# Transposing only the filled partitions: a recurrent attention block with a sparse feed-forward block on one core

## The chip, the cores and the metric

The kernel runs on one core of a Trainium2 chip. The metric is the device time of one execution in microseconds (us), the median of several; lower is better. The profile below is one profiled execution of the same kernel. Its span, from the first to the last instruction, is a little shorter than the device time. Engines are named as the profile names them: PE is TensorE, PEld its weight loads, DVE is VectorE, ACT is ScalarE, POOL is GpSimd, and SPq and ACTq are queues that issue transfers.

## What is computed

The reference runs a decayed outer-product recurrence over 768 steps for 4 batches of 8 heads with head width 48, lays the heads side by side as 384 channels, and passes 128 of each batch's 768 tokens through a two-layer block of hidden width 1024. Cut to what matters:

```python
def _attn_ref(r, k, v, w, u):                      # r, k, v, w: (4, 8, 768, 48)
    for t in range(S):
        cur = np.einsum('bhd,bhe->bhde', u[None] * kt, vt)
        y[:, :, t] = np.einsum('bhd,bhde->bhe', rt, state + cur)
        state = wt[:, :, :, None] * state + np.einsum('bhd,bhe->bhde', kt, vt)

def _moe_ref(x, w_gate, w1, w2, capacity):         # x: (4, 768, 384), w1: (384, 1024), capacity 128
    scores = np.einsum('bsd,d->bs', x, w_gate)
    for b in range(B):
        top_idx = np.argpartition(-scores[b], capacity)[:capacity]
        xe = x[b, top_idx]
        ye = np.maximum(xe @ w1, 0.0) @ w2
        g = 1.0 / (1.0 + np.exp(-scores[b, top_idx]))
        out[b, top_idx] = x[b, top_idx] + g[:, None] * ye
```

All inputs and the output are 4-byte floats.

## The kernel before

The sequence is cut into 24 chunks of 128 tokens, six per batch. A chunk's heads are handled in four pairs (`HP = 4`). Each head takes 64 places (`DP = 64`), of which 48 (`D = 48`) hold data, so that a pair fills 128 partitions: 0 to 47 are the first head, 64 to 111 the second, and 48 to 63 and 112 to 127 are padding. The program is one list of turns; in turn `i` the engines work on chunks `i-2` to `i+2` at different stages. The order of the instructions on each engine is the order of the text.

A transpose is a product on TensorE with the data as the stationary operand and an identity matrix as the moving one. The same helper serves the way in (tokens to channels: `ps_w` for w, `ps_t` for k and r) and the way back (channels to tokens: `ps_t` of `K`, and `ps_y` of `yt`):

```python
    def transposed(pool, tag, src):
        ps = pool.tile([L, HP, L], FP32, tag=tag, name=f"ps_{tag}")
        for j in range(HP - 1, -1, -1):
            nc.tensor.transpose(ps[:, j, :], src(j), ident)       # 128 moving columns
        return ps
```

The way back for the scaled keys gives `kt`, the stationary operand of the products that carry the state:

```python
    def back(t):
        if chunks[t["n"]][1] == NCH - 1:        # a batch's last chunk carries nothing
            return
        ps = transposed(psT, "t", lambda j: t["K"][:, j, :])
        t["kt"] = lev.tile([L, HP, 2, DP], FP32, tag="kt", name="kt")
        nc.scalar.copy(out=t["kt"].rearrange("p j q d -> p j (q d)"), in_=ps)
```

The way back for the results leaves the heads of every second pair in crossed order, so that two instructions take them out:

```python
    def rows_out(t, soon=False):
        b, ci = chunks[t["n"]]
        ps = transposed(psY, "y", lambda j: t["yt"][:, j % 2, j // 2, :])
        y = ps.rearrange("p (a o) (c d) -> p o a c d", o=2, d=DP)
        ...
        for o in (0, 1):
            to = xh[:, o, :, ::-1, :] if o else xh[:, o]
            if soon:                                              # the last two chunks
                ...
                nc.vector.tensor_add(to, y[:, o, :, :, 0:D], ...)
            else:
                nc.scalar.copy(out=to, in_=y[:, o, :, :, 0:D])
        if not soon:
            nc.gpsimd.tensor_add(x, x, vo.rearrange("p h d -> p (h d)"))
        nc.sync.dma_start(out=views[b][b, ci * L:(ci + 1) * L, :], in_=x)
```

Two further helpers use TensorE at the start. `warm` multiplies zeros, and `spread` copies one row into all partitions:

```python
    def warm(n):
        ps = psM.tile([L, 512], FP32, tag="m", name="ps_n")
        for _ in range(n):
            nc.tensor.matmul(ps, nothing[:, 0:L], nothing, start=True, stop=True)

    def spread(to, row):
        ps = psM.tile([L, C], FP32, tag="m", name="ps_b")
        nc.tensor.matmul(ps, one_row, row, start=True, stop=True)
        nc.scalar.copy(out=to, in_=ps)
```

The turn, cut to the calls that the change and the prediction speak of:

```python
    def turn(i):
        soon = i >= N - 1
        ...
        step(scores, i)                    # PE: ps_s
        step(own_values, i)                # ACT: eight sums over rk
        ...
        step(masked, i)                    # DVE: sc
        step(back, i)                      # PE: ps_t <- K; ACT: kt
        if i == 0:
            warm(2)
            spread(wg_bc, wg_row)          # PE: ps_b; ACT: wg_bc
        mix(place="half")
        step(rows_out, i - 1, soon)        # PE: ps_y; ACT or DVE: x; POOL: x
        ...
        fed_in_turn(...)                   # PE: the feed-forward block of an earlier batch
        step(inputs_t, i + 1, "R", r_bufs) # PE: ps_t <- r
        step(scaled, i + 1, "R", "left")   # DVE: R
        step(decays_t, i + 2)              # PE: ps_w <- w
        mix(place="mid")
        if i == -2:
            warm(1)
        ...
        step(outputs_t, i)                 # PE: ps_yt; ACT: yt
        step(carry_products, i)            # PE: ps_kv
        fed_in_turn(...)
        step(inputs_t, i + 2, "K", k_bufs) # PE: ps_t <- k
        if not soon:
            step(row_sums, i - 1)
        step(scans, i + 2)                 # DVE: right_buf, alls, from_left, left
        ...

    warm(6)
    for i in range(-2, N + 1):
        turn(i)
    # then the selection and the feed-forward block of the last batch
```

Of the kernel before, what the change touches and what calls it, by code (L numbers as in the profile page):

```python
# [10 lines left out]
FP32 = mybir.dt.float32  # L11
# [7 lines left out]
L = 128  # L19
DP = 64  # L20
# [18 lines left out]
def kernel(  # L39
# [40 lines left out]
    nc = tc.nc  # L80
    PSUM = bass.MemoryType.PSUM

    B, H, S, D = r.shape
# [4 lines left out]
    HP = H // 2  # L88
    NDC = C // L
    NFC = F // L  # L90
    NHF = NCH // 2
    W = HP * L
    assert S % (2 * L) == 0 and C % L == 0 and F % (4 * L) == 0 and H % 2 == 0
    assert HP % 2 == 0 and D <= DP and W <= 512 and C <= 512 and 0 < CAP < S and CAP % L != 1
    assert B * NCH < 256

    consts = ctx.enter_context(tc.tile_pool(name="consts", bufs=1))
    setup = ctx.enter_context(tc.tile_pool(name="setup", bufs=1))
    lev = ctx.enter_context(tc.tile_pool(name="lev", bufs=2))
    mod = ctx.enter_context(tc.tile_pool(name="mod", bufs=1))  # L100
    psW = ctx.enter_context(tc.tile_pool(name="psW", bufs=1, space=PSUM))
    psT = ctx.enter_context(tc.tile_pool(name="psT", bufs=2, space=PSUM))
    psS = ctx.enter_context(tc.tile_pool(name="psS", bufs=1, space=PSUM))
    psY = ctx.enter_context(tc.tile_pool(name="psY", bufs=1, space=PSUM))
# [9 lines left out]
    def crossed(j, q):  # L114
        return q ^ (j & 1)
# [10 lines left out]
    for queue, hs in ((nc.sync, slice(H // 2, H)), (nc.scalar, slice(0, H // 2))):  # L126
        queue.dma_start(
            out=w_bufs[0][:, hs, 0:D], in_=w[0, hs, 0:L, :].rearrange("h t d -> t h d")
# [23 lines left out]
    def loads(n):  # L152
        load(v_bufs, v, n - 2)
        load(k_bufs, k, n - 1)
        load(r_bufs, r, n - 1)
        load(w_bufs, w, n)
# [19 lines left out]
    def load_weights(n):  # L176
        while n > 0 and weights:
            to, src = weights.pop(0)
            nc.sync.dma_start(out=to, in_=src)
            n -= 1  # L180


    ident = consts.tile([L, L], FP32)
# [7 lines left out]
    high = consts.tile([L, 1], FP32)  # L191
    nc.vector.memset(high, -HIGH)

    row = setup.tile([L, L], INT32)
    nc.gpsimd.iota(row, pattern=[[1, L]], base=0, channel_multiplier=0)
    slots = consts.tile([L, L], BF16)
# [4 lines left out]
    for t, sign in ((before_f, 1), (after_f, -1)):  # L201
        nc.gpsimd.memset(t, 1.0)
        nc.gpsimd.affine_select(
            out=t, in_=t, pattern=[[sign, L]], base=-1, channel_multiplier=-sign,
# [32 lines left out]
# [15 lines that stand above are left out]
        for j in range(HP - 1, -1, -1):  # L252
            nc.tensor.transpose(ps[:, j, :], src(j), ident)  # L253
        return ps

    def decays_t(t):
        wb = w_bufs[t["n"] % NBUF]
        t["wt"] = transposed(psW, "w", lambda j: wb[:, 2 * j:2 * j + 2, :])

    def scans(t):  # L260
# [5 lines left out]
        nc.vector.tensor_tensor_scan(  # L266
            out=flat[:, W - 2::-1], data0=wt[:, W - 1:0:-1],
            data1=from_right.rearrange("p j t -> p (j t)")[:, W - 2::-1], initial=1.0,
            op0=ALU.mult, op1=ALU.max,
# [7 lines left out]
        nc.vector.tensor_tensor_scan(  # L277
            out=left.rearrange("p j t -> p (j t)")[:, 1:W], data0=wt[:, 0:W - 1],
            data1=start.rearrange("p j t -> p (j t)")[:, 1:W], initial=start[:, 0, 0:1],
            op0=ALU.mult, op1=ALU.max,  # L280
# [6 lines left out]
    def check_sums():  # L287

        above = setup.tile([L, 1], FP32)
        nc.vector.tensor_reduce(out=above, in_=guard, axis=AX.X, op=ALU.add)  # L290
        below = setup.tile([L, 1], FP32)
        junk = setup.tile([L, N * HP], FP32)
        nc.vector.tensor_scalar(
            out=junk, in0=alls.rearrange("p n j -> p (n j)"), scalar1=float(LOW ** L),
            scalar2=None, op0=ALU.is_lt, op1=ALU.add, accum_out=below,
        )
        return above, below
# [75 lines left out]
    def back(t):  # L373
        if chunks[t["n"]][1] == NCH - 1:
            return
        ps = transposed(psT, "t", lambda j: t["K"][:, j, :])
        t["kt"] = lev.tile([L, HP, 2, DP], FP32, tag="kt", name="kt")
        nc.scalar.copy(out=t["kt"].rearrange("p j q d -> p j (q d)"), in_=ps)

    state = {}  # L380

# [25 lines left out]

    def rows_out(t, soon=False):
        b, ci = chunks[t["n"]]
        ps = transposed(psY, "y", lambda j: t["yt"][:, j % 2, j // 2, :])  # L410
        y = ps.rearrange("p (a o) (c d) -> p o a c d", o=2, d=DP)
        x = t["x"] = lev.tile([L, C], FP32, tag="x", name="x", bufs=3)
        xh = x.rearrange("p (a o q d) -> p o a q d", o=2, q=2, d=D)
        vo = t.pop("vo")
        for o in (0, 1):
            to = xh[:, o, :, ::-1, :] if o else xh[:, o]
            if soon:
                vh = vo.rearrange("p (a o q) d -> p o a q d", o=2, q=2)
                nc.vector.tensor_add(
                    to, y[:, o, :, :, 0:D], vh[:, o, :, ::-1, :] if o else vh[:, o]  # L420
                )
            else:
                nc.scalar.copy(out=to, in_=y[:, o, :, :, 0:D])  # L423
        if not soon:
            nc.gpsimd.tensor_add(x, x, vo.rearrange("p h d -> p (h d)"))  # L425
        nc.sync.dma_start(out=views[b][b, ci * L:(ci + 1) * L, :], in_=x)

    def row_products(t):
# [211 lines left out]
    def step(f, n, *more):  # L640
        if 0 <= n < N:
            f(work.setdefault(n, dict(n=n)), *more)

    def mix(n=1, place=None):


        while n > 0 and mixing:
            if place is not None and mixing[0][1] not in (None, place):
                return
            try:  # L650
                mixing[0][1] = next(mixing[0][0])
                n -= 1
            except StopIteration:
                mixing.pop(0)
# [16 lines left out]
    def fed_in_turn(n, few):  # L671

        kept = (feed or picked) and (feed or picked)[0][0] == B - 2
        fed(few if kept else n, on=False)
# [6 lines left out]
    def turn(i):  # L681
        soon = i >= N - 1
        step(first_left, i + 1)
        if i < 1:
            step(scaled_aside, i + 1, "K", "right")
        step(own_products, i + 1)
        step(scores, i)
        step(own_values, i)
        step(carry, i - 1, work.get(i))
        if i > 0:  # L690
            step(scaled, i + 1, "K", "right")
        if i >= 0:
            step(own_weights, i + 1)
        if soon:
            step(masked, i)
        if i == N - 1:
            sums.extend(check_sums())
        if i < N:
            step(compared, i - 2)
        if not soon:  # L700
            step(masked, i)
        step(back, i)
        if i == 0:
            warm(2)
            spread(wg_bc, wg_row)
        mix(place="half")
        step(rows_out, i - 1, soon)
        step(row_scores_soon if soon else row_products, i - 1)
        step(own_results, i)
        fed_in_turn(PIECES // 2, 2 if i >= N - 1 else 1)  # L710
        step(inputs_t, i + 1, "R", r_bufs)
        step(scaled, i + 1, "R", "left")
        step(decays_t, i + 2)
        mix(place="mid")
        if i == -2:
            warm(1)
        step(range_check, i + 2)
        if i == -1:
            spread(u_bc.rearrange("p h d -> p (h d)"), u_row)
            step(own_weights, i + 1)  # L720
        step(outputs_t, i)
        step(carry_products, i)
        fed_in_turn(PIECES - PIECES // 2, 1 if i == N - 1 else 0)
        if i == N - 1:
            step(compared, i - 1)
        step(inputs_t, i + 2, "K", k_bufs)
        if not soon:
            step(row_sums, i - 1)
        step(scans, i + 2)
        if 0 <= i - 2 < N - 1 and chunks[i - 2][1] == NCH - 1:  # L730
            mixing.append([mixture(chunks[i - 2][0]), "end"])
        mix(place="end")
        if i > -2:
            loads(i + 5)
        if i in WEIGHT_TURNS:
            load_weights(1)

    with tc.manual_schedule():
# [4 lines that stand above are left out]
        ended.append(True)  # L743
        mix(1000)
        mixing.append([mixture(B - 1), "half"])
        step(compared, N - 1)
        fed(1)
        mix()
        wide = checked(sums)
        fed(1)  # L750
        mix()
        fed(NFC - 2)
        mix(2)
        fed(2)
        mix(1000)
        fed(1000)
        outside = nc.values_load(wide, min_val=0, max_val=1)
# [72 lines left out]
```

## Time and profile before

| what | value |
|---|---|
| device time, three runs | 205.02, 205.38 and 209.82 us; median 205.38 us |
| span of the profiled execution | 203.5 us |
| PE busy | 190.5 us (94%) |
| DVE busy | 161.4 us (79%) |
| POOL busy | 135.5 us (67%) |
| ACT busy | 124.2 us (61%) |
| bytes moved | 28.81 MB, mean 142 GB/s |
| mean granted TensorE clock | 0.996 |

Busy time is the union of an engine's instructions. [...]PE's busy time says how seldom PE had nothing under way, and not what a product costs. That is read from how closely the starts follow each other, or from a piece of the chain of waits. The chain follows the work that ended last back to what released it, step by step; each of its pieces is named by start, duration and instruction. The windows give each engine's busy time in a chosen stretch. Shapes are written partitions x elements.

### The profile page before, as it was taken

Reading aid. Unit: us, or ns where it says so; the run is one execution under the profiler, and the core shown is the slowest. Engines: PE = TensorE matmul, PEld = TensorE weight load, DVE = VectorE, ACT = ScalarE, POOL = GpSimd, SP = SyncE. Lnnn points to the kernel's source line nnn. Section 1 sums busy time; section 2 is a strip of 40 time slices with the busy share of each in tenths; the row PEclk is TensorE's granted clock in tenths of the full one; section 3 lists DMA queues with packets and bytes.
Section 4 is the critical chain, followed back from the end, with each engine's and each line's share of the span. In section 5 each row is a group of like instructions: output and inputs, shape, how many; then the busy total and the mean of one; then the engine's idle time right before and its main releaser. Section 6 shows DMA issues by size and latency. Waiting matters only on the chain.

```text
span 203.5 us, 6413 instructions
## 1 busy us (share of the span) xinstructions
PE 190.5 (94%) x2288; PEld 154.9 (76%) x2289; DVE 161.4 (79%) x357; ACT 124.2 (61%) x642; POOL 135.5 (67%) x167
## 2 busy tenths in 40 slices
PE   6799999989899899999999999999999999999980
PEld 2478888868687788898887888898887888876940
DVE  7979999999999968988879788988879884961010
ACT  4487877768854866878354866878355866510300
POOL 6496898886857996678538898669538898111201
PEclk9999999999999999999999999999999999999998
DMA  7999999999999999798792994998872221111101
GB/s 115 163 163 150 178 192 198 243 210 213 205 216 212 259 230 208 142 244 152 137 158 68 169 183 101 151 162 150 122 116 75 46 79 39 41 42 42 39 8 43
DMA packets 105387, 28.81 MB, mean 142 GB/s; under 512 B 100482, under 2 KB 104580, under 8 KB 105348
## 3 DMA queue, kind: packets, MB, share of 16 engines
q1 hardware_dynamic: 104304, 26.65, 75.1%
q0 software_dynamic: 512, 1.57, 2.5%
q8 instruction: 20, 0.33, 0.8%
q14 instruction: 19, 0.16, 0.3%
q10 hardware_dynamic: 532, 0.10, 0.2%
HBM read 22.81 MB, written 5.51 MB: 139 GB/s over the span
## 4 chain that ended last, share of the span: by engine, by line
PE 85%; DVE 4%; DMA 3%; ACT 2%; POOL 2%; issue 2%; SPq 1%; POOLq 0%; DVEq 0%; ACTq 0%
PE ps_t L253 14%; PE ps_s L360 12%; PE ps_h L606 11%; PE ps_f L618 11%; PE ps_yt L393 11%; PE ps_w L253 5%; PE ps_yt L401 5%; PE ps_y L253 5%; PE ps_kv L455 5%; PE ps_e L496 3%; DMA w_buf<-in_w_dram 3%; PE ps_r L522 1%; PE ps_b L246 1%; ACT rk L345 1%; PE ps_x L570 1%
## 5 line engine op out<-in xcount | busy, mean ns | idle before, releaser
L345 ACT ACTIVATE rk<-rk 128x48 f32<-128x48 f32 x192 | 43.6, 230 | 0.1
L425 POOL TENSOR_TENSOR x<-x,vo 128x384 f32<-128x384 f32 x22 | 22.1, 1004 | 22.5 <-ACT x L423 22.4
L345 ACT ACTIVATION_READ_ACCUMULATOR rk<-rk 128x1 f32 x192 | 36.1, 188 | 0.0
L277 DVE TENSOR_TENSOR_SCAN left<-ps_w,from_left 128x511 f32<-128x511 f32 x24 | 30.7, 1281 | 0.9
L406 ACT COPY yt<-ps_yt 128x512 f32<-128x512 f32 x24 | 14.0, 585 | 28.0 <-PE ps_yt L401 25.2
L368 DVE TENSOR_TENSOR sc<-ps_s,before_f 128x1024 f32<-128x1024 f32 x24 | 29.3, 1219 | 0.8 <-PE ps_s L360 0.8
L266 DVE TENSOR_TENSOR_SCAN right_buf<-ps_w,from_right 128x511 f32<-128x511 f32 x24 | 29.1, 1212 | 0.8 <-PE ps_w L253 0.8
L360 PE MATMUL ps_s<-R,K 48*128 48x128 f32 x384 | 27.9, 285 | 0.3 <-ACT yt L406 0.2
L393 PE MATMUL ps_yt<-sc,v_buf 128*64 128x128 f32 x384 | 26.3, 278 | 1.4 <-PE ps_w L253 1.2
L360 PEld LDWEIGHTS ps_s<-R,K 48*128 48x128 f32 x384 | 23.3, 187 | 3.9 <-issue 2.9
L606 PE MATMUL ps_h<-xeT,w 128*128 128x128 f32 x192 | 25.5, 280 | 0.2 <-ACT hid L611 0.2
L336 POOL TENSOR_TENSOR rk<-r_buf,k_buf 128x384 f32<-128x384 f32 x24 | 24.1, 1006 | 1.3 <-DMA r_buf<-in_r_dram 1.2
L393 PEld LDWEIGHTS ps_yt<-sc,v_buf 128*64 128x64 f32 x384 | 20.6, 136 | 5.7 <-issue 2.9
L339 POOL TENSOR_TENSOR rk<-rk,u_bc 128x384 f32<-128x384 f32 x24 | 24.1, 1003 | 1.3 <-DVE alls L272 0.6
L606 PEld LDWEIGHTS ps_h<-xeT,w 128*128 128x128 f32 x192 | 22.9, 192 | 1.6 <-ACT xeT L572 0.5
L618 PE MATMUL ps_f<-w,hid 128*128 128x384 f32 x64 | 23.8, 499 | 0.0
L430 POOL TENSOR_TENSOR scr<-x,wg_bc 128x384 f32<-128x384 f32 x22 | 22.0, 1001 | 1.7
L351 POOL TENSOR_TENSOR vo<-v_buf,own 128x384 f32<-128x384 f32 x24 | 19.9, 830 | 1.3 <-ACT rk L345 1.3
L324 DVE TENSOR_TENSOR R<-ps_t,left 128x512 f32<-128x512 f32 x24 | 16.5, 687 | 5.0 <-ACT own L584 1.6
L324 DVE TENSOR_TENSOR K<-ps_t,right_buf 128x512 f32<-128x512 f32 x22 | 15.1, 685 | 4.9 <-PE ps_t L253 4.9
L253 PE MATMUL ps_w<-ident,w_buf 128*128 128x128 f32 x96 | 15.0, 278 | 1.5 <-ACT every L507 0.7
L313 ACT ACTIVATE junk<-w_buf,high 128x384 f32<-128x384 f32 x24 | 15.1, 630 | 1.0 <-DMA w_buf<-in_w_dram 0.7
(110 smaller groups left out, 348.1 us busy)
## 6 DMA issues: line engine op xcount, KB each, us to landing
k_buf<-in_k_dram SPq DMA_DIRECT2D x24, 192.0 KB, 4.2
r_buf<-in_r_dram SPq DMA_DIRECT2D x24, 192.0 KB, 4.7
v_buf<-in_v_dram SPq DMA_DIRECT2D x24, 192.0 KB, 4.9
out_dram<-x SPq DMA_DIRECT2D x24, 192.0 KB, 3.5
w_buf<-in_w_dram SPq DMA_DIRECT2D x23, 192.0 KB, 5.0
w<-in_moe_w_dram SPq DMA_DIRECT2D x3, 512.0 KB, 6.0
w<-in_moe_w_dram SPq DMA_DIRECT2D x4, 384.0 KB, 4.8
w_buf<-in_w_dram ACTq DMA_DIRECT2D x1, 96.0 KB
```

The lines of the kernel that those rows point to most:

```text
L253: nc.tensor.transpose(ps[:, j, :], src(j), ident)
L266: nc.vector.tensor_tensor_scan(out=flat[:, W - 2::-1], data0=wt[:, W - 1:0:-1], data1=from_right.rearrange("p j t -> p (j t)")[:, W - 2::- ...
L277: nc.vector.tensor_tensor_scan(out=left.rearrange("p j t -> p (j t)")[:, 1:W], data0=wt[:, 0:W - 1], data1=start.rearrange("p j t -> p (j ...
L324: nc.vector.tensor_mul(out, t.pop(name + "t"), t.pop(by))
L336: nc.gpsimd.tensor_mul(rk, r_bufs[n % NBUF][:, :, 0:D], k_bufs[n % NBUF][:, :, 0:D])
L339: nc.gpsimd.tensor_mul(t["rk"], t["rk"], u_bc)
L345: nc.scalar.activation(out=rk[:, h, :], in_=rk[:, h, :], func=AF.Copy, accum_out=o[:, h:h + 1])
L360: nc.tensor.matmul(ps[:, q, j, :], t["K"][rows, j, :], t["R"][rows, j, :], start=True, stop=True,)
L368: nc.vector.tensor_mul(t["sc"].rearrange("p q j t -> p (q j) t"), ps.rearrange("p q j t -> p (q j) t"), _heads(before_f, 2 * HP),)
L393: nc.tensor.matmul(ps[half(c), j % 2, j // 2, :], vt[:, 2 * j + q, :], t["sc"][:, q, j, :], start=(j < 2), stop=(old is None), skip_group_ ...
L606: nc.tensor.matmul(ps[:, q, :], w1[:, dc, (f0 + q) * L:(f0 + q + 1) * L], xeT[:, dc, :], start=(dc == 0), stop=(dc == NDC - 1),)
L618: nc.tensor.matmul(ps, hid[:, fc, :], w2[:, fc, :], start=(fc == 0), stop=(fc == NFC - 1))
```

## The change

Of the 128 partitions on the way back only 96 hold data, and the last data partition is 111. The change transposes partitions 0 to 111 alone (`DE = DP + D = 112`), with an identity of 112 x 112 whose columns stand in another order: the 48 columns of one head, the 48 of the other, and then the padding between. The result is 112 columns wide, and its first 96 are a pair of heads side by side. A second copy of this matrix has the two heads exchanged, for the crossed pairs. So `x` is taken out by one instruction and not by two, and `kt` by one that copies 384 elements per partition and not 512. As the padding of `kt` is no longer written, `kt` gets two fixed buffers whose padding is set to zero once.

Besides, the products of zeros are placed differently. There are none any more in turn 0 between the transposes of `K` and the row of the gate; at the start, two follow the first transposes of w and one each the first transposes of k and of r.

```diff
+    turned = consts.tile([DE, 2, DE], FP32)
+    for x in (0, 1):
+        for to, src in ((0, DP * x), (D, DP * (1 - x)), (2 * D, D)):
+            n = min(D, DE - to)
+            nc.gpsimd.tensor_copy(out=turned[:, x, to:to + n], in_=ident[0:DE, src:src + n])
+    kt_bufs = [consts.tile([L, HP, 2, DP], FP32, name=f"kt{i}") for i in range(2)]
+    for t in kt_bufs:
+        nc.gpsimd.memset(t[:, :, :, D:DP], 0.0)
 ...
+    def dense(pool, tag, src, order):
+        ps = pool.tile([L, HP, DE], FP32, tag=tag, name=f"ps_{tag}")
+        for j in range(HP):
+            nc.tensor.transpose(ps[:, j, :], src(j), turned[:, order(j), :])
+        return ps[:, :, 0:2 * D]
 ...
     def back(t):
-        ps = transposed(psT, "t", lambda j: t["K"][:, j, :])
-        t["kt"] = lev.tile([L, HP, 2, DP], FP32, tag="kt", name="kt")
-        nc.scalar.copy(out=t["kt"].rearrange("p j q d -> p j (q d)"), in_=ps)
+        ps = dense(psT, "t", lambda j: t["K"][0:DE, j, :], lambda j: 0)
+        t["kt"] = kt_bufs[t["n"] % 2]
+        nc.scalar.copy(out=t["kt"][:, :, :, 0:D], in_=ps.rearrange("p j (q d) -> p j q d", q=2))
 ...
     def rows_out(t, soon=False):
-        ps = transposed(psY, "y", lambda j: t["yt"][:, j % 2, j // 2, :])
 ...                                   (two instructions for x, as shown above)
+        y = dense(psY, "y", lambda j: t["yt"][0:DE, j % 2, j // 2, :], lambda j: crossed(j, 0))
+        xj = x.rearrange("p (j e) -> p j e", j=HP)
+        vo = t.pop("vo").rearrange("p (j q) d -> p j (q d)", q=2)
+        if soon:
+            nc.vector.tensor_add(xj, y, vo)
+        else:
+            nc.scalar.copy(out=xj, in_=y)
+            nc.gpsimd.tensor_add(xj, xj, vo)
 ...
         if i == 0:
-            warm(2)
             spread(wg_bc, wg_row)
 ...
         step(inputs_t, i + 1, "R", r_bufs)
+        if i == -1:
+            warm(1)
 ...
         if i == -2:
-            warm(1)
+            warm(2)
 ...
         step(inputs_t, i + 2, "K", k_bufs)
+        if i == -2:
+            warm(1)
```

More of the change, by code (lines that the diff above doesn't have):

```diff
@@ L92 @@
     W = HP * L
+    DE = DP + D
     assert S % (2 * L) == 0 and C % L == 0 and F % (4 * L) == 0 and H % 2 == 0
@@ L409, in rows_out @@
         b, ci = chunks[t["n"]]
-        ps = transposed(psY, "y", lambda j: t["yt"][:, j % 2, j // 2, :])
-        y = ps.rearrange("p (a o) (c d) -> p o a c d", o=2, d=DP)
+        y = dense(psY, "y", lambda j: t["yt"][0:DE, j % 2, j // 2, :], lambda j: crossed(j, 0))
         x = t["x"] = lev.tile([L, C], FP32, tag="x", name="x", bufs=3)
[L413 to L425, printed above, removed]
+        xj = x.rearrange("p (j e) -> p j e", j=HP)
[5 more added lines that the diff above has]
+            nc.gpsimd.tensor_add(xj, xj, vo)
         nc.sync.dma_start(out=views[b][b, ci * L:(ci + 1) * L, :], in_=x)
```

## The prediction

> **What bounds the kernel now.** I read the busy times first, then the same by stage, then the chain of waits and, where it names an engine, that engine's own instructions. The page's first part calls PE busy for 94% of the span, but this is an average over stages with different limits. So I cut the span at the turns and asked for the busy time by stretch.
>
> ```profile
> core 0: us, PE busy (x) PEld busy (x) DVE busy (x) ACT busy (x) POOL busy (x), PEclk, DMA share, GB/s
> 9.80:16.00 6.20, 5.93 (x70) 4.58 (x70) 4.95 (x9) 4.74 (x26) 5.02 (x5) 1.00 1.53 163
> 16.00:66.00 50.00, 47.61 (x673) 39.58 (x672) 49.02 (x97) 36.70 (x203) 40.02 (x45) 1.00 1.16 202
> 66.00:74.70 8.70, 7.86 (x101) 6.63 (x100) 7.00 (x14) 7.03 (x42) 8.13 (x10) 1.00 1.06 243
> 74.70:171.50 96.80, 96.70 (x1222) 81.43 (x1221) 82.16 (x172) 63.87 (x334) 70.58 (x79) 1.00 0.71 133
> 171.50:203.50 32.00, 25.60 (x203) 19.46 (x203) 10.34 (x39) 6.95 (x29) 6.35 (x8) 0.98 0.12 40
> ```
>
> The reader is to see two regimes. From 16 to 66 us DVE is busy for 49.02 of 50 us and its idle time is slivers: here DVE sets the pace, although PE looks nearly as busy. From 74.7 to 171.5 us, where the feed-forward products of the earlier batches are woven in, PE is busy for 96.70 of 96.80 us while DVE has 14.6 us to spare: here PE sets the pace. The stretch between them is mixed (POOL 8.13 of 8.70). The tail is one serial path.
>
> The chain of waits gives what PE's work costs in the PE stage (turn 10 to 11), and at the end.
>
> ```profile
> 76.12 0.44 PE ps_t L253 x4
> 76.56 0.44 PE ps_y L253 x4
> 76.99 0.67 PE ps_h L606 x6
> ...
> 192.26 5.18 PE ps_f L618 x16
> ```
>
> Four transposes advance the chain by 0.44 us: 0.109 us each, though their records have a mean of 274 ns (each overlaps the next). The second-layer products, 384 columns wide, advance it by 5.18/16 = 0.324 us each.
>
> Last, PE at the start of turn 0, and DVE beside it:
>
> ```profile
> 10.90 0.66 PE L253 MATMUL ps_t<-ident,K 128*128 128x128 f32 x4
> 11.39 0.38 PE L241 MATMUL ps_n<-nothing 128*128 128x512 bf16 x1
> 12.04 0.91 PE L246 MATMUL ps_b<-wg_row,one_row 1*128 1x384 f32 x2 [0.27 <-PE ps_t L253]
> 12.88 0.66 PE L253 MATMUL ps_t<-ident,r_buf 128*128 128x128 f32 x4
> ...
> 11.42 1.20 DVE L368 TENSOR_TENSOR sc<-ps_s,before_f 128x1024 f32<-128x1024 f32 x1
> 13.63 0.69 DVE L324 TENSOR_TENSOR R<-ps_t,left 128x512 f32<-128x512 f32 x1 [1.01 <-PE ps_t L253]
> ```
>
> Two products of zeros (the record of one is missing) stand between 11.39 and 12.04; the row of the gate and the transposes of r queue behind them, and DVE idles 1.01 us for these transposes. It is the last long wait of DVE before its own stage.
>
> [...](324 - 109)/(384 - 128) = 0.84 ns per column for these 4-byte products, and 109 - 128 x 0.84 leaves 1 or 2 ns. [...]The change cuts rows of the stationary operand and columns of the moving one[...]. The trace speaks against this for transposes: their loads have a mean of 141 ns, those of the first-layer products with the same 128 x 128 shape 192 ns, those with 64 columns 137 ns. From the last two a column costs (192 - 137)/64 = 0.86 ns, so a transpose's load is as long as that of about 68 columns, an estimated 58 ns of its 109. The moving side is the longer one. [...]The windows above show the clock at 1.00 from 9.8 us on, so I book no gain for the clock.[...]
>
> **The change, part by part.**
>
> *Narrower transposes.* 20 groups of four for `K` (24 chunks less the last of each batch) and 24 for `yt`. Each transpose loses 16 moving columns: 16 x 0.84 = 13.4 ns, from 109 to about 96. For all 176 this is 2.4 us of PE time, but only a part is on the path. In the PE stage lie turns 10 to 22: 13 groups of `yt`, 11 of `K` (turns 11 and 17 have none), so 96 transposes x 13.4 ns = 1.29 us. From 16 to 66 us the groups lie beside DVE's work: 0. In the tail two groups of `yt` are left: 0.11 us.
>
> *Copies on ACT.* `x` takes two instructions of 128x192 (median 338 ns, some 0.54 us for both, as they overlap) and then one of 128x384; the row copy of that shape, `wg_bc`, takes 0.47 us. `kt` goes from 592 ns at 512 elements to about 0.49 us at 384. About 0.17 us per turn, or 3.5 us of ACT in all; but ACT is busy for 63.87 of 96.80 us in the PE stage and 36.70 of 50 in DVE's. Off the path: 0.
>
> *Additions on DVE in the tail.* Two of 128x192 (0.62 us together) become one of 128x384. DVE's multiplications take 0.34 us at 192 elements and 0.69 at 512, so about 0.55 at 384: 0.07 us in each of two chunks, both on the path from the last results over scores and ranks to the gather. With the narrower `ps_y` there I book 0.2 us for the tail.
>
> *Products of zeros in turn 0.* With none there, the gate's row follows the transposes of `K`. The transposes end some 0.03 us earlier, the change of shape costs what it costs elsewhere (0.20 us from the last transpose's start to the start of `ps_b`), so `ps_b` starts at about 11.45 and not at 12.04. The transposes of r then start at 12.29 and not at 12.88, and DVE's `R` at 13.04 and not at 13.63; `sc` ends at 12.62, so nothing else holds `R`. DVE's chain thus starts its stage 0.59 us earlier. The next input on the way, w of chunk 3, has some 1.2 us in hand. I book 0.55 us.
>
> *Products of zeros between the first transposes.* Before the first transposes of k, r and the second w PE idles about 0.6 us each for a transfer, and one product of 512 columns is shorter than that: hidden, 0.
>
> *Setting up.* Six POOL copies and two fills, each shorter than 0.5 us, before the other tables. POOL's first work on data is at 7.07 us and its set-up ended at 3.84, so some 1.5 us more is hidden: 0.
>
> Sum: 1.29 + 0.2 + 0.55 = 2.04 us. 205.38 - 2.04 = **203.3 us**, or 1.0% less.
>
> **Rivals.**
> - *The loads hold the spacing.* [...]the PE stage gives 0.2 us: 204.4 us. For it: [...]that the first-layer products, with full-length loads, stand at 0.67/6 = 0.112 us. Against it: the 141 ns. I give it one in six.
> - *112 rows cost something.* [...]24 groups in the PE stage lose some 0.1 to 0.2 us each, 2 to 5 us: 206 to 208 us. Nothing in the profile speaks for it; nothing excludes it. One in twelve.
> - *The start's gain is absorbed.* Transfers fill the first 20 us (DMA share 1.53 in turn 0, as packets overlap), and the wait for transposes may turn into one for a transfer of k, r or w: 203.8 us. Against it: the slack that remains. One in four.
> - *A better clock.* If some executions of the kernel before lose the clock at the start, the new places of the zeros help more than this trace tells: 202 or less. One in twenty.
>
> **Range and chances.** The main sum and the absorbed start give 203.3 to 203.8, the loads 204.4; deviations in the mixed stretch are worth some 0.5 us either way. Range **202.2 to 205.0**. A gain of 2% would mean 201.27 us, more than twice the sum[...]. Faster by over 2%: **0.05**, within 2%: **0.91**, slower by over 2%: **0.04**.
>
> **What would show each step.** In the chain of the changed kernel a group of four `ps_y` or `ps_t` from `K` takes 0.38 us and not 0.44[...]. PE's busy time from the start of turn 10 to that of turn 23 falls by 1.3 us and its idle time stays near zero. `R` on DVE in turn 0 starts near 13.0 us, and the distance between the two traces stays near 0.55 us up to 66 us; if it shrinks before, something other than DVE sets that stage. Were the time to fall while DVE's stage gets shorter, or ACT's copies were on a path, my division of stages would be wrong.

## The result and the profile after

| | before | after |
|---|---|---|
| device time, all executions side by side | 205.02, 205.38, 209.66, 209.82 us | 203.42, 203.60, 203.70, 203.95 us |
| median | 207.52 us | 203.65 us |
| span of the profiled execution | 203.5 us | 201.8 us |
| PE busy | 190.5 us | 189.9 us |
| ACT busy | 124.2 us | 121.0 us |
| mean granted clock of the profiled execution | 0.996 | 0.996 |

The ratio after to before is 0.9925 (95% interval 0.9899 to 0.9952); it leaves out the two executions of the kernel before at 209.66 and 209.82 us, while the medians take all; the others are called undisturbed below. So there are two differences to explain: 1.55 us (0.75% of 205.2 us) between undisturbed executions, and a further 2.3 us in the medians, as two of the four executions of before are some 4.5 us above the others and none of the changed kernel's four is (mean clock 0.994 to 0.998).

First the windows of the changed kernel, cut where the same turns begin as in the windows of before. The columns are those of the header line.

```profile
core 0: us, PE busy (x) PEld busy (x) DVE busy (x) ACT busy (x) POOL busy (x), PEclk, DMA share, GB/s
10.00:15.60 5.60, 5.59 (x68) 4.35 (x68) 4.96 (x9) 4.66 (x25) 5.03 (x5) 1.00 1.53 163
15.60:65.50 49.90, 47.07 (x672) 38.87 (x672) 48.92 (x97) 35.52 (x195) 39.84 (x45) 1.00 1.12 201
65.50:74.20 8.70, 7.77 (x101) 6.61 (x100) 7.07 (x14) 6.86 (x41) 8.29 (x10) 1.00 1.04 206
74.20:170.06 95.86, 95.76 (x1221) 80.36 (x1220) 82.10 (x171) 62.09 (x321) 70.61 (x79) 1.00 0.74 140
170.06:201.80 31.74, 25.60 (x203) 19.34 (x203) 10.30 (x37) 6.96 (x29) 6.32 (x8) 0.98 0.12 40
```

The reader is to see that DVE's stage hardly got shorter (48.92 us of DVE in 49.90, against 49.02 in 50) and PE's stage did: from turn 10's first product to turn 23's, 96.76 us became 95.85, and PE is still busy for all but 0.1 us of it. The tail gave 0.25 us (32.01 to 31.76).

Next the chain of waits of the changed kernel in turn 10:

```profile
75.63 0.38 PE ps_t L272 x4
76.01 0.38 PE ps_y L272 x4
76.40 0.68 PE ps_h L618 x6
77.08 0.44 PE ps_t L265 x4
```

The narrow groups (line 272) advance the chain by 0.38 us where they took 0.44. The wide group of r on line 265 keeps 0.44, and so is a control inside the same trace. The product after a narrow group takes 0.68 us where it took 0.67.

Last, DVE near the end of turn 0 in the changed kernel; the bracket is idle time and what ended it:

```profile
11.62 1.20 DVE L387 TENSOR_TENSOR sc<-ps_s,before_f 128x1024 f32<-128x1024 f32 x1
13.21 0.69 DVE L343 TENSOR_TENSOR R<-ps_t,left 128x512 f32<-128x512 f32 x1 [0.40 <-PE ps_t L265]
```

The wait for the transposes of r is 0.40 us instead of 1.01. Yet `R` starts only 0.42 us earlier (13.21 instead of 13.63), because `sc` starts 0.20 us later.

### The profile page after: what moved, and what is told of

The parts are those of the page before. It is cut to its first block, busy times and chain, and to the rows that moved or that the text cites. A ratio compares the mean times of both kernels' runs of the same rounds, so it can differ in the third digit from the quotient of the medians.

```text
span 201.8 us, 6402 instructions
## 1 busy us (share of the span) xinstructions
PE 189.9 (94%) x2290; PEld 153.6 (76%) x2290; DVE 161.2 (80%) x355; ACT 121.0 (60%) x620; POOL 136.7 (68%) x175
## 4 chain that ended last, share of the span: by engine, by line
PE 86%; DVE 5%; ACT 2%; POOL 2%; issue 2%; POOLq 0%; DVEq 0%; ACTq 0%
PE ps_s L379 12%; PE ps_h L618 11%; PE ps_f L630 11%; PE ps_yt L412 11%; PE ps_t L265 9%; PE ps_w L265 6%; PE ps_yt L420 5%; PE ps_kv L467 5%; PE ps_y L272 4%; PE ps_t L272 4%; PE ps_e L508 3%; PE ps_n L253 1%; DVE left L296 1%; DVE right_buf L285 1%; PE ps_r L534 1%
```

## The experiments

Two theories were set against each other. **A:** the gain is PE time in the later turns, plus the earlier `R` at the start; the clock has no part. **B:** most of what the medians show is the clock, which the old placing of the zeros lets fall in some executions. The diffs are against the changed kernel unless a text says otherwise. Beside the changed kernel and the experiments the kernel before ran 96 times: 49 times between 204.96 and 205.73 us and 47 times between 208.33 and 211.43, with nothing between. Where the mean granted clock is on record it was 0.990 to 0.999 in the first group and 0.959 to 0.982 in the second.

### The two halves of the change alone

The new transposes with the zeros placed as before:

```diff
         if i == 0:
+            warm(2)
             spread(wg_bc, wg_row)
         step(inputs_t, i + 1, "R", r_bufs)
-        if i == -1:
-            warm(1)
 ...
         if i == -2:
-            warm(2)
+            warm(1)
 ...
         step(inputs_t, i + 2, "K", k_bufs)
-        if i == -2:
-            warm(1)
```

> The changed kernel with the products of zeros where they were before: two in turn 0, one after the first transposes of w. My theory of three separate terms (PE stage, tail, start): it keeps the PE stage's 0.9 us and the tail's 0.25 us and loses the start's 0.4 us, so about 1.2 us below the kernel before. R in turn 0 starts within 0.1 us of 13.6. If instead the zeros are the whole gain (rival: the narrower transposes are hidden behind DVE's work everywhere), the time is that of the kernel before.

Measured: 204.27, 204.40, 208.53, 208.60, 209.96 and 210.01 us, median 208.56. The narrow transposes alone are worth some 0.9 us, as the lower two against 205.2 show, and four of the six executions are still in the second, upper group of times (mean clock 0.962 to 0.968, against 0.993 and 0.997).

The kernel before with the new placing of the zeros (the opposite edit, on the kernel before):

> The kernel before with the zeros placed as in the changed one, and wide transposes. My theory: about 0.4 to 0.55 us below the kernel before, all of it gained by the end of turn 0 and carried through; PE's stage from turn 10 to turn 23 stays at 96.8 us. Rival (the clock at the start): the zeros between the first transposes keep TensorE's clock up, which is worth more than 1 us at the median, so nearly the whole of the change.

Measured: 204.71 us (204.61 to 204.99 in 15 executions), ratio 0.9977 (0.9968 to 0.9987). The zeros alone are worth 0.5 us of the undisturbed time, and with them none of 15 executions is in the upper group (mean clock 0.991 to 0.999). 0.9 and 0.5 make up the 1.55 us within what such small differences allow.

### Which of the zeros

The kernel before without the two products in turn 0, and nothing put in elsewhere:

```diff
         if i == 0:
-            warm(2)
             spread(wg_bc, wg_row)
```

> The kernel before without its two products of zeros in turn 0, the start's left as it was (one after the first w). My theory: the same 0.4 to 0.55 us as with both moves, since the rest of the zeros is hidden in waits for transfers. Rival (the clock at the start): only a little, under 0.2 us at the median, as the zeros between the first transposes do the work.

Measured: 209.17 us (209.05 to 210.77), ratio 1.0198 (1.0168 to 1.0228): now every execution is in the upper group. Its windows, cut where the clock changes, with the time at half clock in four equal parts:

```profile
4.97:8.38 3.41, 1.87 (x12) 1.21 (x12) 3.15 (x5) 2.03 (x8) 0.97 (x1) 1.00 1.53 163
8.38:11.80 3.42, 3.42 (x13) 1.70 (x13) 3.16 (x5) 0.89 (x4) 2.02 (x3) 0.50 1.53 163
11.80:15.21 3.41, 3.41 (x21) 2.55 (x20) 1.29 (x2) 2.77 (x18) 3.19 (x4) 0.50 1.53 163
15.21:18.62 3.41, 3.41 (x18) 2.30 (x18) 1.32 (x2) 1.08 (x3) 3.05 (x4) 0.50 1.53 163
18.62:22.04 3.42, 3.42 (x34) 3.00 (x32) 2.66 (x6) 2.13 (x16) 0.00 (x0) 0.50 1.52 165
22.04:25.45 3.41, 3.41 (x44) 3.12 (x44) 2.62 (x4) 1.99 (x9) 0.73 (x1) 1.00 1.01 156
```

In the first stretch at full clock PE is busy for 1.87 of 3.41 us, or 55%; then the clock is at half for four such stretches (8.38 to 22.04 us), although PE is busy throughout. Turn 0 takes 10.31 us instead of 6.16, and turn 10 begins at 80.30 us instead of 74.70. The later turns take what they took before. Turn 1 begins at 21.66 us, and in the second experiment, which has the new zeros at the start, at 15.67: the fall cost 6.0 us in this execution, and 4.5 us in the medians (209.17 less 204.71). This is the upper group, seen in a trace. The clock falls at 8.38 us, before the place of the two missing products (11.39 us in the trace of before), so their absence did not start this fall. Why all six executions fell, and only half of those of before, stays open.

The time at half clock is 13.66 us, four times 3.415, and the stretch at full clock before it took 3.41. When full clock first came differs from trace to trace: at 3.93 us in that of before, 4.97 here, 5.20 in the first experiment and 5.76 in the changed kernel.

The kernel before with the new zeros at the start, those of turn 0 kept:

```diff
+        if i == -1:
+            warm(1)                # after the transposes of r
 ...
         if i == -2:
-            warm(1)
+            warm(2)                # after those of w
 ...
+        if i == -2:
+            warm(1)                # after those of k
```

> The kernel before with two, one and one products of zeros after the first transposes of w, k and r, and the two in turn 0 kept. My theory: the time of the kernel before, within 0.2 us; perhaps 0.1 us more where the clock comes up late and the zeros stand in the way of k. Rival (the clock at the start): at least 1 us below the kernel before at the median.

Measured: 205.20 us (204.93 to 205.44 in 14 executions), ratio 0.9994 (0.9985 to 1.0003). The zeros at the start give the undisturbed time nothing, and with them none of the 14 executions is in the upper group (mean clock 0.991 to 0.998). Against the second experiment only the zeros of turn 0 differ. DVE's `R` in this kernel, and then in that one:

```profile
13.83 0.69 DVE L324 TENSOR_TENSOR R<-ps_t,left 128x512 f32<-128x512 f32 x1 [1.01 <-PE ps_t L253]
```

```profile
13.22 0.69 DVE L324 TENSOR_TENSOR R<-ps_t,left 128x512 f32<-128x512 f32 x1 [0.45 <-PE ps_t L253]
```

0.61 us in the trace, and 0.49 us in the medians (205.20 less 204.71): this is what the two products in turn 0 cost.

The changed kernel without any zeros after the first six:

```diff
-        if i == -1:
-            warm(1)
 ...
-        if i == -2:
-            warm(2)
 ...
-        if i == -2:
-            warm(1)
```

> The changed kernel with no product of zeros after the first six. Theory of the clock at the start[...]: the profile shows half the clock from about 8 us to about 20 us and the time is 3.5 to 5 us above the changed kernel, 207 to 209 us. Rival (the falls at the start belong to single executions and not to the order of the program): 203.6 us, as the zeros between the first transposes are hidden in waits for transfers.

Measured: 208.96 us (208.03 to 209.56), ratio 1.0176 (1.0137 to 1.0215). All four executions are over 4 us above the changed kernel, at mean clocks of 0.964, 0.969 and twice 0.995: without zeros the narrow transposes don't keep the time of 203.65, and the new zeros are not idle ballast. The trace shows another form of the loss: here the clock doesn't fall, it comes up only at 20.72 us. The pace tells it, as a group of four wide transposes has a record of 1.11 us shortly before and of 0.66 after:

```profile
16.24 1.11 PE L265 MATMUL ps_t<-ident,r_buf 128*128 128x128 f32 x4
...
20.83 0.66 PE L265 MATMUL ps_t<-ident,k_buf 128*128 128x128 f32 x4
```

The mean granted clock of this execution, 0.995, hides it: the first entry on the clock in the trace is that of 20.72 us, and the time before it counts as full clock, in the column of the windows too. Nor does PE's busy share alone explain it. These are nearly the same stretch of this kernel and of the second experiment:

```profile
3.65:7.06 3.41, 2.84 (x11) 1.86 (x11) 2.45 (x8) 2.11 (x9) 1.44 (x9) 1.00 1.53 164
```

```profile
3.66:7.08 3.42, 3.42 (x14) 2.38 (x14) 2.55 (x8) 2.21 (x9) 0.20 (x2) 1.00 1.52 164
```

With PE busy for 83%, most of it transposes, the clock stayed down; with PE busy throughout and three products of zeros among the transposes it came up at the end of the stretch. Yet 78% (2.66 of 3.41 us), mostly products of zeros, came before the rise at 3.93 us in the trace of before. Whether the gaps or the kind of work made the difference is not shown.

With those after w alone:

```diff
-        if i == -1:
-            warm(1)                # after r
 ...
-        if i == -2:
-            warm(1)                # after k
```

> The changed kernel with only the two products of zeros after the first transposes of w, none after those of k and of r. Theory of the busy share (the clock falls after a window of 3.4 us in which PE was busy for only some 0.55 of it): from 5.2 to 8.6 us PE is again busy for little over half, so the clock falls in part or all of the executions, 207 to 209 us. Rival (any zeros at the start will do): 203.6 us in all.

And with those after k and r alone:

```diff
-        if i == -2:
-            warm(2)                # after w
```

> The changed kernel with one product of zeros each after the first transposes of k and of r, none after those of w. Theory of the busy share: the window from 5.2 to 8.6 us stays above 0.7 busy, and once up the clock doesn't fall; 203.4 to 203.7 us, except where the missing two let the clock come up late. Rival (the zeros after w are what counts): 207 to 209 us.

Measured: 203.64 us for the first (203.47, 203.56, 203.72, and one of 208.09 at a mean clock of 0.970); 203.79 for the second (203.44 to 203.81), with no fall (mean clock 0.990 to 0.997). In the first stretch of 3.41 us at full clock PE is busy for 60% in the first kernel's trace and 70% in the second's, against 63% in the trace of before and 81% in the changed kernel. Whether this share is what decides is not shown: the clock fell after 55% in the third experiment and stayed up after 56% in the profiled execution of the first, whose kernel has four of six executions in the upper group.

Last, transposes of the identity in the place of the zeros, two for each product of 512 columns:

```diff
+    def turn_again(n):
+        ps = psM.tile([L, 512], FP32, tag="m", name="ps_n")
+        for _ in range(2 * n):
+            nc.tensor.transpose(ps[:, 0:L], ident, ident)
 ...
-            warm(1)              # and so at the other two places
+            turn_again(1)
```

> The changed kernel with each product of zeros between the first transposes replaced by two transposes of the identity[...]. [...]the clock falls to half as without zeros, in most executions, and the median is 207 to 209 us. Rival (only the idle time counts): it stays up, 203.6 us.

Measured: 203.62 us (203.49 to 204.13). The loss that one of the two readings foresaw did not come. The trace's stretch after the clock's rise:

```profile
5.88:9.29 3.41, 2.82 (x18) 1.80 (x16) 3.17 (x6) 1.39 (x4) 1.86 (x2) 1.00 1.52 163
```

As fillers, two transposes have a record of 0.38 us, as one product of zeros has, and here they did as well, in four executions (mean clock 0.995 to 0.998): once the clock was up, it stayed up. Whether they also bring it up is not shown; in the kernel without zeros it stayed down over the stretch that was busy for 83%, mostly with transposes.

### Does the narrow shape make the gain, and where

The reordered identity at full size, so that the copies and the additions stay as changed and the transposes have 128 rows and columns again:

```diff
-    turned = consts.tile([DE, 2, DE], FP32)
+    turned = consts.tile([L, 2, L], FP32)
 ...
-        ps = pool.tile([L, HP, DE], FP32, tag=tag, name=f"ps_{tag}")
+        ps = pool.tile([L, HP, L], FP32, tag=tag, name=f"ps_{tag}")
 ...   (and all 128 rows of K and yt)
```

> The changed kernel with the reordered identity at full size, 128 x 128, and all 128 partitions: one instruction for x and 384 elements for kt as in the change, but no narrower transposes. My theory: PE's stage from turn 10 to turn 23 is back at 96.8 us and the time 0.9 to 1.1 us above the changed kernel, 204.6 to 204.8 us; only the additions' 0.15 us of the tail remain. Rival (the fewer and shorter copies on ACT are the gain): the changed kernel's 203.65 us, within 0.2.

Measured: 204.66 us (204.33 to 205.06), 1.0 us above the changed kernel; its PE stage takes 96.76 us, as before. The chain of its turn 10:

```profile
75.67 0.44 PE ps_t L273 x4
76.11 0.44 PE ps_y L273 x4
76.54 0.67 PE ps_h L619 x6
```

Everything is back: 0.44 for the groups, and 0.67 for the product after them. And as this kernel equals the second experiment, which has the old copies (204.71), fewer copies on ACT and fewer additions are worth 0.05 us by the medians, less than their intervals tell apart.

The same extra work in two places: the transposes of `K` are done twice for six chunks of DVE's stage, and for six of PE's (the second pass writes the same results).

```diff
-    def dense(pool, tag, src, order):
+    def dense(pool, tag, src, order, times=1):
-        for j in range(HP):
+        for j in list(range(HP)) * times:
 ...
+                   2 if t["n"] in (2, 3, 4, 6, 7, 8) else 1)        # early
+                   2 if t["n"] in (12, 13, 15, 16, 18, 19) else 1)  # late
```

> The changed kernel with the four transposes of K done twice, into the same place, for chunks 2, 3, 4, 6, 7 and 8: 6 x 0.385 = 2.3 us more of PE's time in DVE's stage. My theory: DVE sets the pace there and PE has 0.1 to 0.5 us in hand per turn, so the time grows by 0 to 0.8 us. Rival (PE sets the pace there too, as its busy share says): the whole 2.3 us.

> The same doubling for chunks 12, 13, 15, 16, 18 and 19, in PE's stage: 2.3 us more of PE's time. My theory: PE sets the pace there and the whole 2.3 us comes on top, 205.9 us. Rival (the two stages don't differ in what sets their pace): the same growth as in the other six chunks.

Measured: 204.16 us early (204.02 to 204.28) and 205.84 late (205.78 to 206.29), so 0.5 and 2.2 us above the changed kernel, for some 2.3 us of work in both. The stage concerned, of the early kernel and then of the late one:

```profile
15.60:59.34 43.74, 42.03 (x600) 35.60 (x599) 42.75 (x79) 32.10 (x177) 36.04 (x40) 1.00 1.17 194
```

```profile
74.26:172.41 98.15, 98.05 (x1245) 82.64 (x1244) 82.10 (x171) 62.46 (x321) 70.61 (x79) 1.00 0.75 138
```

Late, the stage grows from 95.85 to 98.15 us: all of it. Early, the turns 1 to 7 that are shown grow from 43.26 to 43.74 us, and turn 8 not at all: 0.5 us, a fifth, and most of it in turns 2 and 3. The beginning of DVE's stage is not quite free for PE. The change took 0.5 us off PE's busy time in DVE's stage (47.61 to 47.07) and gained nothing there: in that stage more work for PE is felt sooner than less.

### What else could be had

The row of the gate moved behind the transposes of the next w, so that nothing stands between `K` and r:

```diff
         if i == 0:
-            spread(wg_bc, wg_row)
         mix(place="half")
 ...
         step(decays_t, i + 2)
+        if i == 0:
+            spread(wg_bc, wg_row)
```

> The changed kernel with the gate's row copied to all partitions after the transposes of r and w in turn 0, not before them. In the changed kernel DVE still idles 0.40 us for the transposes of r there (R at 13.21, sc done at 12.82). My theory: R starts right after sc, and 0.3 to 0.4 us comes off the whole, 203.3 us. Rival (the inputs still on their way hold turns 0 and 1): under 0.1 us.

Measured: 203.37 us (203.31 to 203.62), ratio to the kernel before 0.9906 (0.9891 to 0.9922). DVE in turn 0:

```profile
11.68 1.20 DVE L387 TENSOR_TENSOR sc<-ps_s,before_f 128x1024 f32<-128x1024 f32 x1
12.79 0.68 DVE L343 TENSOR_TENSOR R<-ps_t,left 128x512 f32<-128x512 f32 x1
```

The wait before `R` is gone, and the total falls by 0.28 us.

Three edits then gave the scores' transposes `ps_e` another bank than that of `ps_w`, because in turns 9, 11 and 17 of the changed kernel `ps_w` seemed to wait for it: in all chunks, the same with the row moved, and with the row moved in all but each batch's first chunk.

```diff
-        ps = psW.tile([L, L], FP32, tag="w", name="ps_e")
+        ps = psK.tile([L, L], FP32, tag="kv", name="ps_e")       # first and second
+        pool, tag = (psK, "kv") if ci > 0 else (psW, "w")        # third
+        ps = pool.tile([L, L], FP32, tag=tag, name="ps_e")
```

> The changed kernel with the scores' transposes (ps_e) in the bank of ps_kv and not in that of ps_w, so that the transposes of w need not wait for ACT's copy of the scores. My theory: PE no longer waits 0.5 us for it in turn 9, and turns 11 and 17 gain the 0.05 us each that the narrower ps_y left there; together 0.3 to 0.6 us off the changed kernel, PE's stage 0.1 us shorter. Rival (another wait takes its place in turn 9): under 0.15 us.

> Both of the edits before in one kernel: the gate's row later, and the scores in the bank of ps_kv. My theory: the two are in different stretches and add up, 0.6 to 1.0 us below the changed kernel, 202.7 to 203.1 us. Rival: one of them only shifts a wait, and the sum is no more than the better one.

> The changed kernel with the gate's row later, and the scores' transposes in the bank of ps_kv only where the selection of a batch does not use that bank in the same turn (chunks 1 to 5 of a batch). My theory: turns 8, 14 and 20 no longer lose what they lost with the bank changed everywhere, turns 11 and 17 keep 0.16 us each and turn 9 some 0.3 to 0.6; with the row's 0.3 us about 202.4 to 202.8 us. Rival (turn 9 is held by the gather and the sums on ACT, not by the bank): 203.0 us.

Measured: 205.97 us (205.63 to 208.90), 205.89 (205.53 to 209.42) and 203.43 (203.26 to 203.59). The first two miss. Turns 11 and 17 do shorten, from 7.03 to 6.87 us each, and turn 9 from 8.72 to 8.01; but turn 8 goes from 6.65 to 7.30, and turns 14 and 20 from 8.04 to 9.18. PE in turn 14 of the first kernel:

```profile
105.37 0.29 PE L508 MATMUL ps_e<-ident,score 128*128 128x128 f32 x1 [0.62 <-DVE mid L482]
105.50 0.55 PE L272 MATMUL ps_t<-turned,K 112*128 112x112 f32 x4
106.44 0.29 PE L558 MATMUL ps_i<-ids,pick 128*128 128x2 bf16 x6 [0.39 <-ACT every L519]
```

The borrowed bank is not free there, and PE, which sets the pace, now idles visibly for 0.62 and 0.39 us. In some executions of these two kernels the time was above 206.5 us at a mean clock of 0.979 to 0.988; no trace of such a one was taken, and its cause is open. The third kernel has the gain of turns 11 and 17 without that loss (PE stage 95.51 us) and gives it back in the tail, 0.44 us longer, where the last batch's ranks wait for the same bank:

```profile
177.90 0.66 PE L535 MATMUL ps_r<-minus,ahead 128*128 128x1 bf16 x21 [0.23 <-DVE ahead L515]
```

So the last chunk got its old bank back (against the third of these kernels):

```diff
-        pool, tag = (psK, "kv") if ci > 0 else (psW, "w")
+        pool, tag = (psK, "kv") if 0 < ci and t["n"] < N - 1 else (psW, "w")
```

> The kernel of the run before (gate's row later, scores by turn) with the scores' transpose of the very last chunk back in the bank of ps_w. In that run the ranks' products (ps_r), which use the bank of ps_kv in the tail, had to wait for the copy of the last scores, 0.39 us. My theory: this wait goes, and the 0.34 us gained in PE's stage come through: 203.0 to 203.1 us. Rival (the tail is held by DVE's comparisons anyway): 203.4 us.

Measured: 202.92 us (202.82 to 203.24), ratio to the kernel before 0.989 (0.9873 to 0.9908), with 95.50 us for the PE stage and 31.64 for the tail. It is the best version of all: 0.7 us below the changed kernel.

## Why the prediction was right or wrong

The time, 203.65 us against 203.3, lies in the range, but the number hides that a cause I set aside was the larger one in the medians. Both theories hold, each for its part: A for the 1.55 us between undisturbed executions, B for the further 2.3 us in the medians.

**The clock: wrong.** The step that failed is "so I book no gain for the clock", with its rival "A better clock" at one in twenty. I took one trace's clock of 1.00 for the kernel's, although one of the three times I had, 209.82, stood 4.4 us above the others. In its place the runs showed that 47 of 96 executions of before are in the upper group, 3.1 to 6.2 us above 205.2, with a mean clock of 0.959 to 0.982 where it is on record. Without the zeros of turn 0 all six executions are there; with the new zeros between the first transposes none is, of 14 with turn 0's zeros and 15 without. I also had the sign in the wrong place: the rival was to show as 202 or less, while it shows as a kernel before whose median is 207.52 and not 205.38. The zeros of turn 0 were not the remedy: with them, half of the executions of before are there. What decides in a single execution is not shown. That a fall of before looks inside like the one in the third experiment is inferred from equal times and clocks; no trace of before with a fall was taken.

**Narrower transposes: right in mechanism, one term too large.** A group fell by 52 ns (0.437 to 0.385 us) where 54 were booked, and two rivals are out. The one on the loads (0.2 us for PE's stage, an estimate of mine that no trace had shown) fails because four transposes in 0.385 us leave 96 ns for each, and not 109, while the loads kept their mean of 141 ns. The one on 112 rows took its 0.1 to 0.2 us per group from the 0.20 us, instead of 0.11, between the last transpose and `ps_b` in the trace of before; in turn 10 each narrow group takes 0.38 us where the wide one took 0.44. But 24 groups by 54 ns, 1.29 us, became 0.91. The trace shows where 0.3 of the missing 0.38 us are. Eleven times the first wide feed-forward product after a narrow group costs 13 ns more: 0.14 us. In turns 11 and 17 a later wait takes 0.04 us each, the rest of what one group gains there. The chain in turn 11, before and after:

```profile
83.83 0.67 PE ps_h L606 x6
...
84.94 0.56 PE ps_w L253 x4
```

```profile
83.20 0.68 PE ps_h L618 x6
...
84.32 0.60 PE ps_w L265 x4
```

`ps_w` had to wait for its bank, as the edits of the bank showed by taking 0.16 us out of this turn. In turns 14 and 20 `ps_i` waits for DVE's choice of tokens and gives back 0.05 us each; this is read from the trace alone. A PE busy for 95.76 of 95.86 us does wait: while one product waits, the record of the one before still runs (272 ns for a transpose of `ps_w`, with 109 ns between starts).

**Zeros of turn 0: right, and nearly in size.** Booked 0.55 us; 0.49 in medians and 0.61 in traces where the edit stands alone. In the profiled pair it came to 0.42 at `R`, because the clock happened to rise 1.8 us later: the first transposes of w took 1.09 us and not 0.74, and DVE's chain began late. The offset then stayed, and is 0.43 us at the start of turn 8 (turns 1 to 7 take 43.32 us before and 43.26 after), as the division of stages said. The rival "The start's gain is absorbed" is out.

**Zeros between the first transposes: right in time (0.9994), wrong in meaning.** They cost nothing in undisturbed time, and with them none of 29 executions is in the upper group.

**Copies, additions, setting up, tail: right.** ACT lost 3.2 us of work without a trace in the total. The tail gave 0.25 us where 0.2 were booked; its chain shows 0.10 from two narrow groups and 0.08 from one addition that ends earlier, and the tails of kernels with the same work there differ by as much as the rest (31.87 us in the second experiment, 32.01 before, 32.08 in the fourth).

Together: 0.91 in PE's stage, 0.25 in the tail, 0.43 up to turn 8 and 0.05 in the mixed stretch make 1.64 of the 1.66 us between the spans.

## What to carry to other kernels

Before pricing a change to a kernel whose times fall in two groups, ask which group the profile belongs to and what the clock does in the other: work that looks useless at the start may hold it up (203.65 us with four products of zeros there, 208.96 without), and here transposes did as well as products of zeros (203.62 us). A mean clock near 1 can hide a late start (0.995 with the rise at 20.72 us); compare the duration of the same instructions early and late (1.11 and 0.66 us). A saved product is worth its full time only where its engine sets the pace (2.3 us of added work cost 2.2 us in PE's stage and 0.5 in DVE's), and even there a later wait on a bank takes some back (0.04 us in turn 11); follow the chain to the next wait for another engine. To move a tile to another bank, look at all stages that use that bank, not only the one that waits (turns 11 and 17 gained 0.16 us each, turns 14 and 20 lost 1.14 each).

## What the runs showed of the hardware that was not expected

- In one trace (the third experiment) a stretch of 3.41 us with PE busy for 55% was followed by half the clock, which lasted 13.7 us, four such stretches, although PE was busy throughout by its records. This cost 6.0 us in that execution.
- In another (the changed kernel without zeros) the clock came up only at 20.72 us, although PE was busy for 83% of the stretch from 3.65 to 7.06 us and for 90% of the next (3.08 of 3.42 us).
- As fillers between the first transposes, transposes of the identity did as well as products of zeros: 203.62 us with the first (mean clock 0.995 to 0.998), 203.65 with the second (0.994 to 0.998), 208.96 with neither (0.964 to 0.995).
- Transposes of 112 rows and 112 columns start 96 ns after each other, those of 128 and 128 after 109 ns. The first group of six feed-forward products behind the narrow ones takes 13 ns more (0.68 us instead of 0.67); transposes of 128 rows right behind them keep their 0.44 us.
